# Reordered group work in the first expert layer of an FFT convolution with two dense layers, on one core

## The chip, the cores and the metric

The kernel runs on one core of a Trainium2 chip. The metric is the device time of one execution in microseconds (us), lower is better. The core's engines are TensorE (PE in the profile; its weight loads are PEld), VectorE (DVE), ScalarE (ACT), GpSimd (POOL), and SyncE (SP), which here only issues transfers. Each engine works through its own queue in the order of the program; an instruction that waits holds back all that stands behind it in the same queue.

## The reference

`x` has the shape (2, 3008, 256). It is filtered along the sequence by a product of Fourier transforms, and the 6016 tokens then pass two dense layers with 2048 hidden units each.

```python
X = np.fft.rfft(x, axis=1)
y = np.fft.irfft(X * (filt_r + 1j * filt_i), n=3008, axis=1)
x = y.reshape(6016, 256)
h = x @ moe_w_in                                   # 256 -> 2048
g = where(h >= 1, h, where(h <= -1, 0, (h + 1)**2 / 4))
x = g @ moe_w_out                                  # 2048 -> 256
h = x @ moe2_w_in
g = h / (1 + exp(-h))
return g @ moe2_w_out
```

The weights of both layers come as 64-bit floats, read as pairs of words. Every product is made from operands that are split in two rounded parts, high (h) and low (l): three matmuls, high by high, high by low and low by high, stand for one.

## The kernel before, in words

**Stages.** The first 340 us hold the transforms, the weights of the first layer and the first half of that layer's tokens, one unit of 128 hidden columns and about 500 tokens per slot of the agenda (`up`, `act_rest`, `split_g`, `down`). From slot `GA` (368.92 us in the profiled execution) on, the work goes in *groups*: nine pairs of token blocks (`PL`: three pairs of the first layer, `p` 0 to 2, then six of the second, `p` 3 to 8) times eight pairs of hidden units (`j`), so 72 groups, called G0 to G71 here (G = 8p + j). G0 to G23 are the first layer's, called wide; G24 to G71 the second layer's.

**A group (`group`, line 607).** Seven products in Strassen's manner stand for the eight block products of a pair of token blocks with a pair of hidden units. They are made in three PSUM banks `b`, `d`, `c` out of a ring of four (tag `h` of the pool `hp`; `load_pair` and `up` use the same ring): the first product and two more add up in `b`, two in `c`, one in `d`. Between them stand bank copies on ACT (`snap`: s1, u2, u4, line 546) and additions on DVE (c11 line 623, c22 line 661, c21 line 678), which give the four blocks 11, 22, 12 and 21. PE's order in a group is A11 and A12 into b and d, two matmul sets of the previous group's block 11 (line 387 on, six matmuls), S2 into b, block 22's six, S3 into c, S1 into b, block 12's six, S4 into b, A22 into c, block 21's six: 45 matmuls. S4 into b follows the copy u4; A22 into c follows the addition c22; the next group's d takes the bank that this group's b had, so it follows the last reading of b, which is block 12's activation.

**A block's chain (`Chain`).** `first` (ACT, line 565), `square` (ACT, 569), `last` (DVE, 574), `high` (the rounding, ACT, 582) and `low` (the remainder, DVE, 585); the block's six matmuls take the outputs of the last two. In a wide group the chains of blocks 22, 12 and 21 end in the next group. The blocks lie in a ring of three buffers (`block`, line 549).

**The agenda.** `at(t, fn)` puts a function at slot `t`; `due(t)` issues it. In the groups a group has four slots, and `between[i]` issues one block's six matmuls and then what is due in slot `GA + 4 * G + i`. What stands there: the first layer's weight sums (`sum_first` on DVE: six additions; `round_first` on ACT: two roundings; `rest_first` on POOL: two remainders), the same for the second layer's weights (`get_weight`: transfers on SP's queue; `sum_weight`, `round_weight`, `rest_weight`: four additions, three roundings, three remainders), and the next pair's tokens (`load_pair`, `sum_x` on DVE line 523, `split_x2` on ACT line 528, `rest_x2` on DVE line 533). The weights' staging tiles (tag `wa`) are a ring of three buffers.

**Around G0.** `up` and `down` slots GA - 16 to GA - 1 hold one unit each, 12 matmuls. DVE has in each slot the remainder gl (line 375) and the activation g (line 367), which frees a bank of the ring; the last four of these banks become b, d, c of G0 and b of G1. The same stretch also holds the last four weight conversions of the second layer (`form_weight`, lines 179 to 182, three DVE and one POOL instruction each, in slots GA - 10, - 8, - 6 and - 4), and the first pair's loading, sums and splits.

**Evictions.** When a pair's last group is done, its two output blocks are copied out (`evict`, line 391): each as one copy on ACT with its store on ACT's queue, and one on DVE with its store on SP's. The copies lie in a ring of four buffers (tag `ob`), from which each pair's operand T2 takes one too.

Of the kernel before, what the change touches and what calls it, by code (L numbers as in the profile page):

```python
# [9 lines left out]
F32 = mybir.dt.float32  # L10
# [82 lines left out]
def tile_fft_conv_moe_moe(  # L93
# [297 lines left out]
    def evict(o, name, to):  # L391
        for e in range(2):
            ob = mp.tile([128, PMAX], F32, tag="ob", name=f"ob{name}_{e}", bufs=4)[:, :o[e].shape[1]]
            if e == 0:
                nc.scalar.activation(ob, o[e], AF.Copy)  # L395
                nc.scalar.dma_start(to[e], ob)
            else:
                nc.vector.tensor_copy(ob, o[e])
                nc.sync.dma_start(to[e], ob)
# [91 lines left out]
    def load_pair(p):  # L491
        m, q = PL[p]
        n = size(p)
        for k in range(2):
            xstage[p, k] = mp.tile([128, 2 * n], F32, tag="x", name=f"xs{p}_{k}")
            if m == 1:
                t0 = BLOCKS[2 * q][0]
                nc.sync.dma_start(xstage[p, k], x2d[k, :, t0:t0 + 2 * n])
        if m == 0:
            for i in range(2):  # L500
                for k in range(2):
                    to = xstage[p, k][:, i * n:(i + 1) * n]
                    ps = last_stage(2 * q + i, k)
                    if k == 0:
                        nc.scalar.activation(to, ps, AF.Copy)
                    else:
                        nc.vector.tensor_copy(to, ps)

    def operand(p, which):

        n = size(p)
        if which == "T2":
            if (p, which) not in xstage:
                xstage[p, which] = mp.tile([128, PMAX], F32, tag="ob", name=f"t2_{p}", bufs=4)
            return xstage[p, which][:, :n]
# [33 lines left out]
    def block(p, j, name):  # L549
        return late.tile([128, PMAX], F32, tag="c", name=f"c{name}{p}_{j}", bufs=3)[:, :size(p)]  # L550

# [55 lines left out]
    def group(p, j, prev, between):  # L607
# [8 lines left out]
        if pwide:  # L616
            prev["22"].high()
            prev["22"].low()
            prev["12"].high()
# [3 lines left out]
        nc.vector.tensor_tensor(c11, d, s1, ALU.add)  # L623
        if pwide:
            prev["12"].low()
        if prev:
# [21 lines left out]
        k11.last()  # L648
        if pwide:
            prev["21"].high()  # L650
        between[1]()
        c = bank(p, j, "c")
        prod(c, p, j, "S3", "T3", True)
        prod(b, p, j, "S1", "T1", False)
        u4 = snap(b, p, j, "u4")
        if wide:
            k11.high()
        if pwide:
            prev["21"].low()
        c22 = block(p, j, "22")  # L660
        nc.vector.tensor_tensor(c22, c, u4, ALU.add)  # L661
        if wide:
# [86 lines left out]
    for j in range(NP):  # L749
        at(GA - 4 + 4 * j, sum_first, j)  # L750
        at(GA - 3 + 4 * j, round_first, j)
        at(GA - 2 + 4 * j, rest_first, j)
    zw = []
# [22 lines left out]
    for j in range(NP):  # L776
        t = Y - 24 + 4 * j + (4 if j > 2 else 0)
        for i in range(2):
            at(t - 2 + i, get_weight, 2 * j + i)
        at(t, sum_weight, j)  # L780
        at(t + 1, round_weight, j, store)
        at(t + 2, rest_weight, j)

# [12 lines left out]
    at(GA - 14, make_ring)  # L796
    first = {"B11": -11, "B21": -10, "T2": -7, "T3": -5, "T1": -3, "B22": -1, "T4": 0}
    sums = {"T1": -9, "T2": -8, "T3": -6, "T4": -1}
    later = {"B11": 12, "B21": 14, "T2": 18, "T3": 28, "T1": 28, "B22": 29, "T4": 30}
    sums_later = {"T1": 16, "T2": 17, "T3": 20, "T4": 24}  # L800
    for p in range(len(PL)):
        t = GA + 4 * NP * (p - 1) if p else GA
        at(t + (3 if PL[p][0] else 7) if p else GA - 12, load_pair, p)
        for which, d in (sums_later if p else sums).items():
# [125 lines left out]
```

## Time and profile before

| | |
|---|---|
| three runs, us | 1163.71, 1163.79, 1160.23 (median 1163.71) |
| the profiled execution's own time, us | 1160.99 |
| its span from the first to the last instruction, us | 1159.2 |
| mean granted TensorE clock, as a share of full speed | 0.996 |
| PE busy, us | 1120.9 |
| ACT busy, us | 818.7 |
| DVE busy, us | 771.3 |

The profile is of one execution. A line of a timeline has the start and the length of an instruction in us, its engine, its line in the kernel, the operation, output and inputs with shapes, and how many stand behind one another (x2); in square brackets is the idle time of the engine just before it and what ended it. PE matmuls overlap: consecutive ones start about 0.227 us apart and are shown 0.39 us long.

### The profile page before, as it was taken

What the parts mean: (1) busy time and instruction counts of PE and PEld (TensorE: products, weight loads), DVE (VectorE), ACT (ScalarE), POOL (GpSimd) and SP (SyncE); (2) the same over time, 40 slices, a digit from 0 to 9 for tenths busy, and PEclk for the clock granted to TensorE, in tenths of its full rate; (3) what the DMA queues carried; (4) which work ended last, traced back from release to release, by engine and by line L of the source; (5) the groups of instructions that cost most, each with busy time, mean ns of one, the idle gap of its engine ahead of it and who ended that gap; (6) DMA issues with size and microseconds to landing.
All of it is one profiled execution on the core that took longest, in us unless ns stands there. A gap on an engine that the chain in (4) does not pass through costs nothing.

```text
span 1159.2 us, 14143 instructions
## 1 busy us (share of the span) xinstructions
PE 1120.9 (97%) x4931; PEld 903.5 (78%) x4931; DVE 771.3 (67%) x1226; ACT 818.7 (71%) x1515; POOL 250.8 (22%) x220
## 2 busy tenths in 40 slices
PE   9899999999998998999999899999999999999998
PEld 4477787878887876788777678888888888888887
DVE  7977657878759788767778765545555555555443
ACT  3588777878866677878888776666666666666655
POOL 5677535657512111000021320000000000000000
PEclk9999999999999999999999999999999999999999
DMA  9732042444231000000120120110200200200000
GB/s 239 207 107 94 1 129 69 134 123 135 82 110 55 19 0 1 36 1 1 54 82 19 33 103 1 37 35 1 72 1 1 72 1 1 72 1 1 36 1 35
DMA packets 35591, 63.67 MB, mean 55 GB/s; under 512 B 4064, under 2 KB 18624, under 8 KB 35520
## 3 DMA queue, kind: packets, MB, share of 16 engines
q1 hardware_dynamic: 31808, 56.38, 16.2%
q10 hardware_dynamic: 3712, 6.40, 1.5%
q8 instruction: 38, 0.62, 0.2%
q14 instruction: 33, 0.27, 0.1%
HBM read 46.25 MB, written 16.52 MB: 54 GB/s over the span
## 4 chain that ended last, share of the span: by engine, by line
PE 77%; DVE 9%; ACT 7%; DMA 2%; issue 2%; POOL 2%; SPq 0%; DVEq 0%; ACTq 0%; POOLq 0%
PE o L387 13%; PE o L389 12%; PE o L388 12%; PE b L537 5%; PE b L538 5%; PE b L539 5%; PE h L354 3%; PE h L356 3%; PE h L355 3%; PE c L537 3%; PE xp L326 2%; PE c L538 2%; PE c L539 2%; DVE gl L585 1%; ACT gh L582 1%
## 5 line engine op out<-in xcount | busy, mean ns | idle before, releaser
L387 PE MATMUL o<-gh,wh 128*128 128x502 f32 (+1 forms) x624 | 245.4, 393 | 0.5 <-ACT ob L395 0.3
L389 PE MATMUL o<-gh,wl 128*128 128x502 f32 (+1 forms) x624 | 244.8, 392 | 0.0
L388 PE MATMUL o<-gl,wh 128*128 128x502 f32 (+1 forms) x624 | 244.6, 392 | 0.0
L585 DVE TENSOR_TENSOR gl<-c,gh 128x502 fp32r<-128x502 f32 (+1 forms) x288 | 195.5, 693 | 61.4 <-ACT gh L582 60.9
L582 ACT ACTIVATE gh<-c 128x502 fp32r<-128x502 f32 (+1 forms) x288 | 170.2, 617 | 11.7 <-DVE c L574 8.9
L546 ACT ACTIVATE u<-b 128x502 f32<-128x502 f32 (+1 forms) x144 | 83.8, 582 | 95.9 <-PE b L539 95.7
L387 PEld LDWEIGHTS o<-gh,wh 128*128 128x128 f32 x624 | 118.5, 190 | 26.4 <-ACT ob L395 1.0
L389 PEld LDWEIGHTS o<-gh,wl 128*128 128x128 f32 x624 | 118.3, 190 | 24.8
L388 PEld LDWEIGHTS o<-gl,wh 128*128 128x128 f32 x624 | 118.5, 190 | 24.3
L661 DVE TENSOR_TENSOR c<-c,u 128x502 f32<-128x502 f32 (+1 forms) x72 | 48.9, 679 | 100.9 <-ACT u L546 100.9
L561 ACT ACTIVATE c<-c 128x502 f32<-128x502 f32 (+1 forms) x144 | 88.6, 616 | 26.8 <-DVE c L661 26.2
L375 DVE TENSOR_TENSOR gl<-g,gh 128x502 fp32r<-128x502 f32 (+1 forms) x80 | 64.7, 809 | 51.5 <-ACT gh L373 51.4
L373 ACT ACTIVATE gh<-g 128x502 fp32r<-128x502 f32 (+1 forms) x96 | 59.8, 622 | 54.8 <-PE o L389 32.2
L678 DVE TENSOR_TENSOR c<-c,u 128x502 f32<-128x502 f32 (+1 forms) x72 | 48.9, 680 | 68.8 <-PE c L539 68.6
L546 ACT ACTIVATE s<-b 128x502 f32<-128x502 f32 (+1 forms) x72 | 42.5, 590 | 68.9 <-PE b L539 68.9
L354 PE MATMUL h<-xh,wh 128*128 128x502 f32 (+1 forms) x192 | 76.7, 399 | 3.8 <-DVE g L367 3.8
L367 DVE SCALAR_TENSOR_TENSOR g<-u,h 128x502 f32<-128x502 f32 (+1 forms) x96 | 64.2, 669 | 23.8 <-ACT u L366 23.8
L356 PE MATMUL h<-xh,wl 128*128 128x502 f32 (+1 forms) x192 | 75.1, 391 | 1.3 <-POOL wl L198 1.3
L355 PE MATMUL h<-xl,wh 128*128 128x502 f32 (+1 forms) x192 | 74.9, 390 | 0.0
L623 DVE TENSOR_TENSOR c<-d,s 128x502 f32<-128x502 f32 (+1 forms) x72 | 49.0, 680 | 32.9 <-PE d L539 23.8
L182 POOL TENSOR_TENSOR wa<-wa,raw 128x512 int32<-128x512 int32 x32 | 50.3, 1573 | 78.9 <-DVE wa L181 34.8
L360 ACT ACTIVATE u<-h 128x502 f32<-128x502 f32 (+1 forms) x96 | 55.5, 578 | 13.0 <-PE h L356 12.5
(197 smaller groups left out, 2405.0 us busy)
## 6 DMA issues: line engine op xcount, KB each, us to landing
f<-in_filt_dram SPq DMA_DIRECT2D x64, 192.0 KB, 4.6
raw<-in_moe_w_in_dram SPq DMA_DIRECT2D x32, 256.0 KB, 2.7
raw<-in_moe_w_out_dram SPq DMA_DIRECT2D x32, 256.0 KB, 3.1
w2d<-wa SPq DMA_DIRECT2D x16, 256.0 KB, 3.4
wb<-w2d SPq DMA_DIRECT2D x16, 256.0 KB, 2.8
xs<-x2d SPq DMA_DIRECT2D x8, 502.0 KB, 4.9
Z<-in_x_dram SPq DMA_DIRECT2D x16, 192.0 KB, 6.1
x<-in_x_dram SPq DMA_DIRECT2D x16, 192.0 KB, 3.6
```

Of the source, the lines that this page charges most:

```text
L354: nc.tensor.matmul(h, wh[:, s], xh[:, k, :t], start=(k == 0), stop=False)
L355: nc.tensor.matmul(h, wh[:, s], xl[:, k, :t], start=False, stop=False)
L356: nc.tensor.matmul(h, wl[:, s], xh[:, k, :t], start=False, stop=(k == 1))
L387: nc.tensor.matmul(o[e], wh[:, s], gh, start=first, stop=False)
L388: nc.tensor.matmul(o[e], wh[:, s], gl, start=False, stop=False)
L389: nc.tensor.matmul(o[e], wl[:, s], gh, start=False, stop=last)
L537: nc.tensor.matmul(bank, wh, xh, start=first, stop=False, skip_group_check=True)
L538: nc.tensor.matmul(bank, wh, xl, start=False, stop=False, skip_group_check=True)
L546: nc.scalar.activation(v, src, AF.Copy)
L561: nc.scalar.activation(self.g, self.h, AF.Silu)
L582: nc.scalar.activation(self.gh, self.g, AF.Copy)
L585: nc.vector.tensor_tensor(self.gl, self.g, self.gh.bitcast(F32), ALU.subtract)
```

## The change

In a group that follows a wide one, the remainder of the previous group's block 22 goes behind the addition c11, the rounding of its block 21 behind the copy u4, and the remainder of that block behind the addition c22. The block buffers become four and the eviction buffers three. `sum_first`, `round_first` and `rest_first` go from slots 0, 1, 2 of the group before (for j = 0: GA - 4, - 3, - 2) to slots 0, 2, 3 of the group before that one (j = 0: GA - 14, - 11, - 10; j = 1: GA - 6, - 5, - 4). `sum_weight` and its followers go from eight of the nine groups G18 to G26 (one per group, none in G21) to G18, G20, G22, G24, G25, G26, G27 and G28, the rounding in slot 2 in place of 1 and the remainder in slot 3 in place of 2. The first pair's loading goes from one slot to two, one slot earlier, and its sums and splits go earlier by one to six slots.

```diff
@@ -390,7 +390,7 @@
 
     def evict(o, name, to):
         for e in range(2):
-            ob = mp.tile([128, PMAX], F32, tag="ob", name=f"ob{name}_{e}", bufs=4)[:, :o[e].shape[1]]
+            ob = mp.tile([128, PMAX], F32, tag="ob", name=f"ob{name}_{e}", bufs=3)[:, :o[e].shape[1]]
             if e == 0:
                 nc.scalar.activation(ob, o[e], AF.Copy)
                 nc.scalar.dma_start(to[e], ob)
@@ -496,22 +496,24 @@
             if m == 1:
                 t0 = BLOCKS[2 * q][0]
                 nc.sync.dma_start(xstage[p, k], x2d[k, :, t0:t0 + 2 * n])
-        if m == 0:
-            for i in range(2):
-                for k in range(2):
-                    to = xstage[p, k][:, i * n:(i + 1) * n]
-                    ps = last_stage(2 * q + i, k)
-                    if k == 0:
-                        nc.scalar.activation(to, ps, AF.Copy)
-                    else:
-                        nc.vector.tensor_copy(to, ps)
+
+    def load_block(p, i):
+
+        n = size(p)
+        for k in range(2):
+            to = xstage[p, k][:, i * n:(i + 1) * n]
+            ps = last_stage(2 * PL[p][1] + i, k)
+            if k == 0:
+                nc.scalar.activation(to, ps, AF.Copy)
+            else:
+                nc.vector.tensor_copy(to, ps)
 
     def operand(p, which):
 
         n = size(p)
         if which == "T2":
             if (p, which) not in xstage:
-                xstage[p, which] = mp.tile([128, PMAX], F32, tag="ob", name=f"t2_{p}", bufs=4)
+                xstage[p, which] = mp.tile([128, PMAX], F32, tag="ob", name=f"t2_{p}", bufs=3)
             return xstage[p, which][:, :n]
         i, half = {"B11": (0, 0), "B12": (0, 1), "B21": (1, 0), "B22": (1, 1),
                    "T1": (0, 0), "T3": (0, 1), "T4": (1, 0)}[which]
@@ -547,7 +549,7 @@
         return v
 
     def block(p, j, name):
-        return late.tile([128, PMAX], F32, tag="c", name=f"c{name}{p}_{j}", bufs=3)[:, :size(p)]
+        return late.tile([128, PMAX], F32, tag="c", name=f"c{name}{p}_{j}", bufs=4)[:, :size(p)]
 
     class Chain:
 
@@ -615,13 +617,13 @@
         s1 = snap(b, p, j, "s1")
         if pwide:
             prev["22"].high()
-            prev["22"].low()
             prev["12"].high()
         d = bank(p, j, "d")
         prod(d, p, j, "A12", "B21", True)
         c11 = block(p, j, "11")
         nc.vector.tensor_tensor(c11, d, s1, ALU.add)
         if pwide:
+            prev["22"].low()
             prev["12"].low()
         if prev:
             prev["21"].first()
@@ -646,19 +648,19 @@
         if pwide:
             prev["21"].last()
         k11.last()
-        if pwide:
-            prev["21"].high()
         between[1]()
         c = bank(p, j, "c")
         prod(c, p, j, "S3", "T3", True)
         prod(b, p, j, "S1", "T1", False)
         u4 = snap(b, p, j, "u4")
+        if pwide:
+            prev["21"].high()
         if wide:
             k11.high()
+        c22 = block(p, j, "22")
+        nc.vector.tensor_tensor(c22, c, u4, ALU.add)
         if pwide:
             prev["21"].low()
-        c22 = block(p, j, "22")
-        nc.vector.tensor_tensor(c22, c, u4, ALU.add)
         if wide:
             k11.low()
         between[2]()
@@ -747,9 +749,10 @@
     GA = NB + W1S
     Y = GA + 4 * NP * (len(PAIRS) - NS // 2)
     for j in range(NP):
-        at(GA - 4 + 4 * j, sum_first, j)
-        at(GA - 3 + 4 * j, round_first, j)
-        at(GA - 2 + 4 * j, rest_first, j)
+        t, r = ((GA - 14, 3), (GA - 6, 1))[j] if j < 2 else (GA + 4 * (j - 2), 2)
+        at(t, sum_first, j)
+        at(t + r, round_first, j)
+        at(t + r + 1, rest_first, j)
     zw = []
 
     def store(j):
@@ -774,12 +777,12 @@
         at(t + 3, form_weight, 1, f)
         at(t + 5, put_weight, f)
     for j in range(NP):
-        t = Y - 24 + 4 * j + (4 if j > 2 else 0)
+        t = Y - 24 + 8 * j if j < 3 else Y + 4 * (j - 3)
         for i in range(2):
             at(t - 2 + i, get_weight, 2 * j + i)
         at(t, sum_weight, j)
-        at(t + 1, round_weight, j, store)
-        at(t + 2, rest_weight, j)
+        at(t + 2, round_weight, j, store)
+        at(t + 3, rest_weight, j)
 
     def make_ring():
         xr = zp.tile([128, 8, 2, 512], F32R, tag="z0", name="xr")
@@ -794,13 +797,17 @@
         ring.extend(lambda i=i: extra(i) for i in range(2))
 
     at(GA - 14, make_ring)
-    first = {"B11": -11, "B21": -10, "T2": -7, "T3": -5, "T1": -3, "B22": -1, "T4": 0}
-    sums = {"T1": -9, "T2": -8, "T3": -6, "T4": -1}
+    first = {"B11": -12, "B21": -11, "T2": -8, "T3": -6, "T1": -5, "B22": -3, "T4": -2}
+    sums = {"T1": -10, "T2": -9, "T3": -8, "T4": -7}
     later = {"B11": 12, "B21": 14, "T2": 18, "T3": 28, "T1": 28, "B22": 29, "T4": 30}
     sums_later = {"T1": 16, "T2": 17, "T3": 20, "T4": 24}
     for p in range(len(PL)):
         t = GA + 4 * NP * (p - 1) if p else GA
-        at(t + (3 if PL[p][0] else 7) if p else GA - 12, load_pair, p)
+        s = t + (3 if PL[p][0] else 7) if p else GA - 13
+        at(s, load_pair, p)
+        if PL[p][0] == 0:
+            for i in range(2):
+                at(s + (0 if p else i), load_block, p, i)
         for which, d in (sums_later if p else sums).items():
             at(t + d, sum_x, p, which)
         for which, d in (later if p else first).items():
```

## Rows read from the trace of the kernel before

**Rows 1.** The page's first part: busy time of an engine, share of the span, instructions.

```profile
PE 1120.9 (97%) x4931; PEld 903.5 (78%) x4931; DVE 771.3 (67%) x1226; ACT 818.7 (71%) x1515; POOL 250.8 (22%) x220
```

**Rows 2.** The waits of PE: line, what it waited for, us in total, times, longest us.

```profile
PE b L537 <- ACT u L546: 15.0, 13, 1.6
...
PE c L537 <- DVE c L661: 2.6, 3, 1.4
```

**Rows 3.** Busy time by stretch: from:to, length, then busy time (instructions) of PE, PEld, DVE, ACT, POOL, granted clock, DMA share, GB/s. The stretches begin at the first matmul of G0, G1, G2, G8, G16, G18 and G24; the last one ends with G26.

```profile
368.92:386.53 17.61, 14.64 (x53) 11.49 (x51) 15.46 (x26) 11.70 (x24) 5.28 (x5) 0.81 0.04 16
386.53:403.76 17.23, 16.31 (x99) 14.07 (x97) 11.19 (x21) 10.59 (x21) 1.51 (x2) 1.00 0.08 30
403.76:474.08 70.32, 63.79 (x273) 50.16 (x272) 57.60 (x106) 55.39 (x107) 9.26 (x10) 1.00 0.00 1
474.08:563.71 89.63, 88.80 (x410) 73.03 (x408) 65.17 (x104) 71.24 (x132) 0.00 (x0) 1.00 0.03 12
563.71:584.08 20.37, 20.37 (x91) 16.93 (x90) 15.85 (x26) 17.36 (x33) 0.00 (x0) 1.00 0.43 140
584.08:655.66 71.58, 64.05 (x271) 51.00 (x270) 58.58 (x99) 59.55 (x112) 21.05 (x15) 0.98 0.12 34
655.66:689.10 33.44, 31.32 (x136) 25.06 (x135) 21.00 (x39) 25.23 (x47) 11.18 (x9) 1.00 0.27 93
```

**Rows 4.** The chain of work that ended last, in order of time: start, us, step. One step of it, the 48 small matmuls of a pair's loading.

```profile
333.88 5.30 PE xp L326 x48
```

**Rows 5.** Timeline of G17, a group with nothing due: first matmul, the copy u4, S4's first matmul, and block 12's last DVE step.

```profile
573.91 0.38 PE L537 MATMUL b<-xr,wh 128*128 128x500 f32 x1
...
580.21 0.59 ACT L546 ACTIVATE u<-b 128x500 f32<-128x500 f32 x1
...
581.36 0.39 PE L537 MATMUL b<-xr,sh 128*128 128x500 f32 x1
...
583.58 0.67 DVE L574 SCALAR_TENSOR_TENSOR c<-v,b 128x500 f32<-128x500 f32 x1
```

**Rows 6.** Timeline of G3, a group with a weight sum: its first matmul, the sum's first additions, the last steps of blocks 21 and 11, the rounding of block 21, the first of the weight's two roundings, the copy u4, and S4's first matmul.

```profile
415.24 0.38 PE L537 MATMUL b<-xr,wh 128*128 128x502 f32 x1
...
419.23 0.76 DVE L451 TENSOR_TENSOR wr<-wh,wl 128x256 f32<-128x256 f32 x2
...
421.27 1.27 DVE L574 SCALAR_TENSOR_TENSOR c<-v,c 128x502 f32<-128x502 f32 x2
421.98 0.62 ACT L582 ACTIVATE gh<-c 128x502 fp32r<-128x502 f32 x1 [0.87 <-DVE c L574]
...
422.51 0.51 ACT L441 ACTIVATE sh<-ws 128x384 fp32r<-128x384 f32 x1
423.12 0.57 ACT L546 ACTIVATE u<-b 128x502 f32<-128x502 f32 x1
...
423.74 0.50 PE L537 MATMUL b<-xr,sh 128*128 128x502 f32 x1 [0.83 <-ACT u L546]
```

**Rows 7.** Timeline in G15 (a token rounding ahead of u4, two token remainders ahead of c22, A22's first matmul) and in G18 (a second-layer weight's three roundings on ACT and its first two remainders on POOL).

```profile
558.80 0.60 ACT L528 ACTIVATE xr<-xs 128x500 fp32r<-128x500 f32 x1
559.01 1.26 DVE L533 TENSOR_TENSOR xr<-xs,xr 128x500 fp32r<-128x500 f32 x2
...
561.51 0.50 PE L537 MATMUL c<-xr,wh 128*128 128x502 f32 x1 [0.62 <-DVE c L661]
...
590.47 1.13 ACT L441 ACTIVATE wz<-wb 128x512 fp32r<-128x512 f32 x2
591.16 2.53 POOL L444 TENSOR_TENSOR wz<-wb,wz 128x512 fp32r<-128x512 f32 x2 [130.58 <-ACT wz L441]
591.51 0.51 ACT L441 ACTIVATE sh<-ws 128x384 fp32r<-128x384 f32 x1
```

**Rows 8.** Timeline around the first matmuls of G0, DVE, POOL and PE: two remainders gl with DVE's idle time before each, the POOL addition of the last weight conversion, the remainder gl beside that, a POOL remainder, the activation g of slot GA - 3, and d's first matmul.

```profile
358.30 0.68 DVE L375 TENSOR_TENSOR gl<-g,gh 128x500 fp32r<-128x500 f32 x1 [0.75 <-ACT gh L373]
...
365.19 0.68 DVE L375 TENSOR_TENSOR gl<-g,gh 128x500 fp32r<-128x500 f32 x1 [0.75 <-ACT gh L373]
...
370.05 1.51 POOL L182 TENSOR_TENSOR wa<-wa,raw 128x512 int32<-128x512 int32 x1 [7.32 <-DVE wa L181]
370.33 1.75 DVE L375 TENSOR_TENSOR gl<-g,gh 128x500 fp32r<-128x500 f32 x1
371.52 1.43 POOL L444 TENSOR_TENSOR sl<-ws,sh 128x384 fp32r<-128x384 f32 x1
372.01 0.66 DVE L367 SCALAR_TENSOR_TENSOR g<-u,h 128x500 f32<-128x500 f32 x1
...
372.73 0.79 PE L537 MATMUL d<-xr,wh 128*128 128x502 f32 x1 [2.97 <-DVE g L367]
```

**Rows 9.** Busy time by stretch behind that matmul (columns as in rows 3).

```profile
373.70:378.40 4.70, 4.70 (x13) 3.71 (x12) 4.29 (x8) 3.83 (x8) 0.00 (x0) 0.50 0.00 0
```

**Rows 10.** Timeline: the idle time of PE ahead of S4 in G24.

```profile
664.84 0.49 PE L537 MATMUL b<-xr,sh 128*128 128x502 f32 x1 [1.50 <-ACT u L546]
```

**Rows 11.** Timeline of the end: the store of the first of the last four copies, and the last copy on DVE.

```profile
1154.03 0.34 ACTq L396 DMA_DIRECT2D out_dram<-ob_11p  x1
...
1155.44 0.68 DVE L398 COPY ob_10p<-o 128x500 f32<-128x500 f32 x1 [0.67 <-PE o L389]
```

**Rows 12.** The list of transfers: queue, count, KB each, us from issue to landing.

```profile
out_dram<-ob_11p ACTq DMA_DIRECT2D x1, 250.0 KB, 2.0
```

## The prediction

> **What bounds the kernel now.** The busy shares come first [rows 1]: PE is busy for 1120.9 us of a span of 1159.2, so at most some 38 us can be won without fewer matmuls, and the change takes none away. Next, who ends PE's idle times [rows 2]: 13 waits of S4 into b for the copy u4 on ACT take 15.0 us, 3 waits of A22 into c for the addition c22 take 2.6. Last, where: the stretches from G0 to G26 [rows 3]. G16 and G17 take 20.37 us, 10.2 a group, 45 matmuls without a gap; a pair's loading adds 5.3 [rows 4]. What each stretch has above that is the excess:
>
> G0: 17.61 less 51 matmuls of 0.227 (11.6) is 6.0. G1: 17.23 - 10.2 - 5.3 = 1.7. G2 to G7: 70.32 - 61.2 = 9.1. G8 to G15: 89.63 - 81.6 - 5.3 = 2.7. G16, G17: none. G18 to G23: 71.58 - 61.2 = 10.4. G24 to G26: 33.44 - 30.6 = 2.8. Together 32.7 us: all that the change can touch, since nothing it moves lies later, but for the buffers.
>
> The mechanism is read from a quiet and a loaded group. In G17 u4 starts 6.30 after the group's first matmul, and S4 7.45 after it, on time [rows 5]. In G3 u4 starts at 7.88 and S4 0.83 late [rows 6]: DVE's weight sum holds it from 3.99 to 6.03, so the last step of block 21 comes late, its rounding ends an ACT idle time of 0.87 at 6.74, the weight's roundings follow, and u4 stands behind all of them. PE waits for an order of work, not for a full engine: in G2 to G7 ACT is busy for 55.39 of 70.32 us, DVE for 57.60 [rows 3].
>
> **The change part by part.** *Copy u4 ahead of block 21's rounding, weight roundings to slot 2.* In G1 to G24 ACT can start u4 as soon as b is done, at 6.3; it takes 0.59, and S4 is due at 7.45. So the wait of S4 goes, with 0.5 to spare. c22 follows at 6.95 to 7.6, A22 is due at 8.15.
>
> What is late next is the start of d. Block 12's last step reads b, and the next group's d takes that bank. In G17 block 12's last DVE step ends at 10.34 [rows 5]; d is due at 10.2 + 0.68 = 10.88, so 0.54 is spare. Whatever now stands on ACT between the rounding of block 11 and block 22's first step (R) moves that chain. Where R is over 0.54, d is late by R - 0.54, and I add 0.15 for the restart. A first-layer weight's two roundings are 0.61 (422.51 to 423.12) [rows 6]: a wait of 0.2. With one token rounding (0.60, of which 0.53 start to start) it is 0.75. A second-layer weight's three are 1.55 (590.47 to 592.02) [rows 7]: 1.15; with a token rounding 1.7.
>
> By group: G1 keeps 0.4, since the next pair's loading stands ahead of G2's d. G2 and G5 0.2 each, G3 and G4 0.75 each (a token rounding is due in their slot 2), G6 has no weight left, G7 below: 2.6 in place of 9.1 with G7. G18 1.15, G19 0, G20 1.7, G21 0, G22 1.15. G24 has 0.5, its chain's second-layer form reading b in its first step; G25 and G26 none, where the roundings stand behind u4 and ACT is less full (25.23 of 33.44 us) [rows 3]: 0.5 in place of 2.8.
>
> *Token splits.* In G7, G15 and G23 two token remainders (1.26 on DVE) precede c22 and a token rounding (0.60) precedes u4 [rows 7]. Neither moves. In G15 A22 starts 0.62 late; block 21's remainder (0.6) stood behind the two and goes behind c22, but what the splits themselves cost ACT and DVE stays, and with it the start of the next d. I keep 0.7 in each of the three, of bounds 0.1 and 1.3. With 0.6 for the small rests in G8 to G14, G8 to G15 keep 1.3; G18 to G23 keep 1.15 + 1.7 + 1.15 + 0.7 = 4.7.
>
> *Block 22's remainder behind c11, block 21's behind c22.* Nothing is added; each comes later by one or two DVE steps of 0.6 to 0.7. Block 22's low matmuls are due at 3.63 and its remainder would end at about 2.85; block 21's are due at 9.07 and its remainder would end at 8.2. Cost nothing while that cover of 0.8 holds; without it, see the slower rival. The fourth block buffer is what lets c11 go ahead of the remainder that frees the buffer of block 22.
>
> *A port shared by DVE and POOL.* A POOL addition at 370.05 lasts until 371.56, and the remainder gl that DVE issues at 370.33 takes 1.75 in place of 0.68; the activation g with one input in PSUM takes its normal 0.66 beside POOL's next remainder [rows 8]. The Trainium skill, SBUF — State Buffer, "Who interferes with whom", says that whichever of the two starts first holds the shared pair for its whole instruction when DVE has two SBUF inputs, and that a DVE operation with one does not contend. By that rule the weights' remainders, now issued at about 8.4, would delay block 11's remainder only if it started after them; I have it at 8.15, so nothing. Were it the other way round, c21 and block 12's last step would come behind it, 0.35 in each of some nine groups: 3 us more.
>
> *Around G0.* d waits for g of slot GA - 3, 2.97 us [rows 8]. Between slot GA - 10 and that g DVE keeps four weight conversions, four token remainders and one weight sum (j = 1's for j = 0's) and gets one token sum more (0.6). The weight sum comes two slots sooner and fills DVE's two idle times of 0.75: -1.5. A POOL remainder now falls before that g and can hold a DVE remainder: between 0 and 1.43 [rows 8]; I take 0.5. So g is 0.4 earlier, bounds 0.9 earlier (POOL holds nothing) and 2.0 later (no idle time filled, POOL's whole 1.43), and PE idles for 2.6. Behind the 2.97 the granted clock was 0.50 of full, 1.2 GHz, for 13 matmuls and more [rows 9], which makes the other 2.9 of the 6.0; behind a single 1.50 in G24 PE goes on without such a stretch [rows 10], and the stretch of G24 to G26 has a clock of 1.00 [rows 3]. 2.6 is nearer to 2.97: I let the clock fall, and G0 keeps 5.6. If it does not, 2.9 more are won.
>
> *Eviction buffers, three.* Each pair's fourth copy now takes the buffer of its first and waits for that store. At the end of a pair's other groups the two are some 3 us apart, and a store lands after 2.0 [rows 12]: no wait. Behind the last matmul they are not: store issued at 1154.03, landed at 1156.03, the copy was at 1155.44 [rows 11]. The end comes 0.6 to 0.7 later; I take 0.7.
>
> **Sum.** What stays is 5.6 + 0.4 + 2.6 + 1.3 + 4.7 + 0.5 + 0.7 = 15.8, against 32.7: 16.9 less. The profiled execution's own time is 1160.99 (span 1159.2 and 1.8 around it); it lies 2.7 below the median of the three runs and beside the lowest. 1160.99 - 16.9 = 1144.1; I forecast 1144.
>
> **The rivals.** *The waits move to d and are no shorter (14 in 100).* If ACT's steps behind u4 come later than I have them, or POOL holds DVE as above, d waits for block 12 in every loaded group. G2 to G7 keep 5, G18 to G23 8, G0 its 6.0: 15.8 + 2.4 + 3.3 + 0.4 + 1 = 22.9 stays, 1151. For it: S4's wait today covers d's. Against it: the idle ACT time of 0.87 in front of block 21's rounding is gone in any case.
>
> *The clock stays up in G0 and d's waits are hidden (10 in 100).* G0 keeps 2.7 and the waits for d half: about 9 stay, 1137. For it: the first pair's work begins sooner. Against: no less DVE work before that g.
>
> *The stalls are work, not order (7 in 100).* Then ACT is late whatever the order, and the time stays between 1158 and 1164. Against it stand the quiet groups and the busy times [rows 3].
>
> *The deferred remainder of block 21 comes too late (7 in 100): slower.* Its low matmuls stand at the end of each group. From 0.9 later than my 8.2, PE waits there; every group from G1 to G24 pays, the nine quiet ones too. At 0.7 of wait a group, 24 x 0.7 = 16.8 eat the whole gain; at 1.0 the time is 1144 + 24 = 1168. For it: it now stands behind u4, two roundings and c22. Against: ACT and DVE are idle for parts of that stretch in G17.
>
> **How the numbers follow.** The forecast has 62 in 100, from 1138 to 1150 with the clock in G0 and the bounds above. A difference of 0.3% (3.5 us) is about what can be told here. Faster is the forecast and the first two rivals, 86; the same 7; slower 7. The range 1136 to 1156 leaves out the last two and the far end of the second, some 17 in 100.
>
> **What would show it.** Right: no wait of PE for u4 in G1 to G23, waits of about 1 to 1.7 of d for block 12's last step in G19, G21 and G23 (behind G18, G20, G22), half a granted clock after d in G0 still, a last DVE copy that waits for a store. Wrong: waits in front of block 21's low matmuls, any gap in G16 or G17, or waits of d behind groups without weight work.

## The result, and the profile after

The changed kernel takes 1143.93 us (median of four runs, 1143.57 to 1145.48), the kernel before beside it 1163.53 (1160.23 to 1163.79): a ratio of 0.9841, 95% interval 0.9821 to 0.9861. The prediction was 1144, range 1136 to 1156, with 86 in 100 for faster. The profiled execution takes 1143.57 us against 1160.99, so 17.4 less, where 16.9 was worked out. The sum is right; its terms are not all, as the stages show.

The windows by stage of the changed kernel stand in the same order as [rows 3]: G0, G1, G2 to G7, G8 to G15, G16 and G17, G18 to G23, G24 to G26; then G0 to G26 together, and from G27 to the end.

```profile
369.51:385.52 16.01, 12.11 (x52) 9.47 (x51) 13.04 (x23) 10.92 (x23) 3.10 (x3) 1.00 0.05 17
385.52:401.52 16.00, 16.00 (x98) 14.21 (x97) 10.73 (x21) 10.35 (x20) 1.68 (x2) 1.00 0.09 33
401.52:465.24 63.72, 62.62 (x273) 50.78 (x273) 53.96 (x99) 55.19 (x105) 7.87 (x8) 1.00 0.00 1
465.24:553.58 88.34, 88.04 (x410) 73.19 (x409) 64.46 (x104) 70.79 (x132) 0.00 (x0) 1.00 0.04 12
553.58:574.12 20.54, 20.54 (x91) 16.83 (x90) 16.16 (x27) 17.31 (x33) 0.00 (x0) 1.00 0.41 139
574.12:638.89 64.77, 62.89 (x272) 50.23 (x270) 50.59 (x88) 55.94 (x106) 11.13 (x9) 1.00 0.07 21
638.89:671.09 32.20, 31.49 (x137) 25.22 (x135) 22.15 (x41) 24.82 (x48) 10.94 (x9) 1.00 0.34 108
369.51:671.09 301.58, 293.69 (x1323) 239.92 (x1321) 231.10 (x398) 245.32 (x463) 34.72 (x31) 1.00 0.10 32
671.09:1141.80 470.71, 466.15 (x2050) 386.00 (x2048) 250.50 (x393) 303.91 (x551) 8.33 (x7) 1.00 0.07 24
```

The first number behind the window is its length; less 10.2 for each group (11.58 for G0, and 5.3 more where a pair is loaded) it gives the excess, as in the prediction:

| stage | before | predicted | after |
|---|---|---|---|
| G0 | 6.0 | 5.6 | 4.4 |
| G1 | 1.7 | 0.4 | 0.5 |
| G2 to G7 | 9.1 | 2.6 | 2.5 |
| G8 to G15 | 2.7 | 1.3 | 1.4 |
| G16, G17 | 0 | 0 | 0.1 |
| G18 to G23 | 10.4 | 4.7 | 3.6 |
| G24 to G26 | 2.8 | 0.5 | 1.6 |
| together | 32.7 | 15.1 | 14.1 |

That is 18.6 less in G0 to G26 (320.18 us before, 301.58 after). The part from G27 on takes 0.6 more (470.10 before), and G0 starts 0.6 later (368.92 before): 18.6 - 0.6 - 0.6 = 17.4. That G0 starts later is no work of the change: the first matmul of `up` starts at 58.66 before and at 59.38 after, so the shift is there long ahead of the first slot that the change touches. In the profiles of the kernels below G0 starts between 368.2 and 374.7, whatever their edit. Experiments are therefore compared by the length of G0 to G26, and totals by their medians.

What PE waits for in G0 to G26 answers to [rows 2]. The columns are the total in us, how many times, the longest.

```profile
PE d L539 <- DVE g L367: 2.3, 1, 2.3
PE c L539 <- DVE c L661: 2.2, 5, 0.7
...
PE b L539 <- issue: 1.6, 1, 1.6
...
PE o L388 <- DVE gl L587: 0.6, 1, 0.6
...
PE b L539 <- ACT u L548: 0.4, 1, 0.4
...
PE b L539 <- ACT s L548: 0.3, 1, 0.3
```

The wait for the copy u4, 13 times and 15.0 us before, is there once, for 0.4, in G23. The addition c22 is waited for five times, 2.2 in all (G4, G7, G15, G23, G25). d waits once, in G0 and for g; there is no wait of d for block 12, which the prediction had put into ten groups.

G3 shows what became of the mechanism in [rows 6]. Its timeline after the change (the group's first matmul is at 411.88):

```profile
418.23 0.59 ACT L548 ACTIVATE u<-b 128x502 f32<-128x502 f32 x1 [0.47 <-PE b L541]
...
418.72 1.12 ACT L584 ACTIVATE gh<-c 128x502 fp32r<-128x502 f32 x2
...
419.39 0.39 PE L539 MATMUL b<-xr,sh 128*128 128x502 f32 x1
```

u4 starts at +6.35, where it was +7.88, and what ends ACT's idle time in front of it is PE's last matmul into b: it is as early as it can be. Block 21's rounding follows behind it as one of the two at 418.72, and S4 comes at +7.51 with no idle time in front.

### The profile page after: what moved, and what is told of

The parts are those of the page before. It is cut to its first block, busy times and chain, and to the rows that moved or that the text cites. A ratio compares the mean times of both kernels' runs of the same rounds, so it can differ in the third digit from the quotient of the medians.

```text
span 1141.8 us, 14135 instructions
## 1 busy us (share of the span) xinstructions
PE 1114.9 (98%) x4931; PEld 901.7 (79%) x4931; DVE 765.1 (67%) x1226; ACT 817.0 (72%) x1515; POOL 249.5 (22%) x220
## 4 chain that ended last, share of the span: by engine, by line
PE 82%; DVE 6%; ACT 4%; issue 2%; POOL 1%; DMA 0%; ACTq 0%; DVEq 0%; SPq 0%; POOLq 0%
PE o L388 14%; PE o L387 14%; PE o L389 14%; PE b L539 5%; PE b L541 5%; PE b L540 5%; PE h L354 3%; PE c L539 3%; PE h L356 3%; PE h L355 3%; PE c L541 3%; PE c L540 3%; PE xp L326 3%; PE d L539 1%; PE d L540 1%
## 5 line engine op out<-in xcount | busy, mean ns | idle before, releaser
L587 DVE TENSOR_TENSOR gl<-c,gh 128x502 fp32r<-128x502 f32 (+1 forms) x288 | 191.0, 691 | 40.0 <-ACT gh L584 39.8
L576 DVE SCALAR_TENSOR_TENSOR c<-v,c 128x502 f32<-128x502 f32 (+1 forms) x72 | 49.2, 690 | 22.7 <-ACT v L571 22.4
```

What stands on the lines that cost most here:

```text
L587: nc.vector.tensor_tensor(self.gl, self.g, self.gh.bitcast(F32), ALU.subtract)
```

## Experiments

Ten runs follow. The first three tell apart where the gain comes from, the next five test the places where something was left, and the last two put together what helped and repeat the changed kernel.

**1. The order inside the groups alone.** The kernel before with the new order in `group` and the new buffer counts; the agenda stays as it was.

```diff
             prev["22"].high()
-            prev["22"].low()
             prev["12"].high()
...
         u4 = snap(b, p, j, "u4")
+        if pwide:
+            prev["21"].high()
         if wide:
             k11.high()
+        c22 = block(p, j, "22")
+        nc.vector.tensor_tensor(c22, c, u4, ALU.add)
         if pwide:
             prev["21"].low()
```

> The kernel before with the new order inside a group and the new buffer counts, its agenda left as it was. Theory (order): PE waited because u4 stood behind block 21's rounding; with u4 ahead, the waits of S4 for u4 in G1 to G6 nearly go although the weight sums and roundings stay in their old slots. Left: G0's 6.0, some 0.5 for each second-layer weight whose three roundings (1.45) still stand ahead of u4, 0.8 at the end. About 20 of the 32.7 us of excess stay: 1148, between 1145 and 1152. Rival (agenda): the weight work in the same group is what costs; then this run stays within 4 us of the kernel before, 1156 to 1161.

Measured: 1152.81 us (1151.47 to 1153.45), ratio 0.9930, interval 0.9914 to 0.9947. G0 to G26 take 310.89 us: 9.3 of the 18.6. The waits of PE in that stretch, as above:

```profile
PE c L537 <- DVE c L659: 5.1, 8, 1.3
...
PE b L537 <- ACT u L546: 3.3, 5, 1.6
```

Most of the 13 waits for u4 go by the order alone. But 8 waits for c22 with 5.1 us take the place of 3 with 2.6. In G3 to G6 they do not come from u4, which starts there at +6.4, on time: DVE is late. Out of G3:

```profile
419.13 1.22 POOL L444 TENSOR_TENSOR sl<-ws,sh 128x384 fp32r<-128x384 f32 x1 [8.67 <-PE b L539]
419.15 0.57 ACT L546 ACTIVATE u<-b 128x502 f32<-128x502 f32 x1
...
419.39 1.50 DVE L533 TENSOR_TENSOR xr<-xs,xr 128x502 fp32r<-128x502 f32 x1
...
420.81 0.67 DVE L659 TENSOR_TENSOR c<-c,u 128x502 f32<-128x502 f32 x1
```

A token remainder on DVE starts 0.26 behind a POOL remainder of the weight, which the old agenda has in slot 2, and takes 1.50 where two take 1.26 elsewhere [rows 7]. c22 follows it without idle time, 1.09 after the end of u4. In G0 to G26 of this run 24 steps of DVE last over 0.8 us, together some 17 us more than at their usual 0.67; in the kernel before there are 16 with some 8 us, in the changed kernel 6 with some 4. That is DVE's time and not PE's, but it shows what the agenda adds here: it takes POOL's remainders out of the way of the steps ahead of c22. In G18 to G25 the second-layer roundings in slot 1 stand ahead of u4 as well. The expectation was too good.

**2. The agenda alone.** The other half: the changed kernel with the old order in `group` and the old buffer counts.

```diff
+            prev["22"].low()
             prev["12"].high()
...
+        if pwide:
+            prev["21"].high()
         between[1]()
...
         u4 = snap(b, p, j, "u4")
-        if pwide:
-            prev["21"].high()
```

> The changed kernel with the old order inside a group and the old buffer counts: the agenda's moves alone. Theory (order): with a weight sum still in slot 0, u4 comes at about 7.3 behind block 21's rounding and S4 waits some 0.5 in each of G1 to G5, 1.0 where a token sum stands there too; the second-layer weights gain by being spread. About 18 us of excess stay: 1146, between 1143 and 1151; the two parts alone add up to more than the change, since either removes the roundings from ahead of u4. Rival (the order does it all): within 3 us of the kernel before.

Measured: 1152.09 us (1151.43 to 1155.48), ratio 0.9933, interval 0.9918 to 0.9949; G0 to G26 308.40, so 11.8 of the 18.6. Waits for u4 remain six times with 3.1, for c22 eight times with 3.7, so this expectation, too, was too good. Neither half is the change: 9.3 + 11.8 = 21.1 against 18.6 together, so each takes away some of the stalls that the other would. The rival, under which the agenda alone gives almost nothing, falls.

**3. The second layer's weights back in their old slots.** All else as changed.

```diff
-        t = Y - 24 + 8 * j if j < 3 else Y + 4 * (j - 3)
+        t = Y - 24 + 4 * j + (4 if j > 2 else 0)
...
-        at(t + 2, round_weight, j, store)
-        at(t + 3, rest_weight, j)
+        at(t + 1, round_weight, j, store)
+        at(t + 2, rest_weight, j)
```

> The changed kernel with the second layer's weight sums, roundings and remainders in their old slots. Theory: three roundings of together 1.45 stand ahead of u4 again, in six groups, two of them on end with token splits; G18 to G26 go from some 5 us of excess to 9 to 11: 1148 to 1150. Rival: the new order gives ACT room enough, and the spread is worth under 1.5: 1143 to 1145.

Measured: 1150.67 us (1149.80 to 1154.26), ratio 0.9921, interval 0.9905 to 0.9937. G18 to G26 take 102.49 us against 64.77 + 32.20 = 96.97, so 5.5 more; G0 to G17 take 204.61 in both. The waits in G0 to G26:

```profile
PE c L539 <- DVE c L661: 3.4, 5, 1.3
...
PE b L539 <- ACT u L548: 3.3, 5, 1.6
```

The u4 waits come back, 3.3 in place of 0.4, in the loaded groups of that stage alone. With the roundings in slot 1 the order u4 first doesn't help, since they stand ahead of it. So 5.5 of the 18.6 hang on where this work stands. The run moves the slots and the groups together and doesn't tell them apart.

**4. The last four weight conversions moved out of G0's approach**, into slot 3 of the groups G8 to G11, which have no weight work. Their raw words now all go through the one buffer with the tag `raw`.

```diff
+        elif m == 1:
+            raw = rawp.tile([128, 512], I64, tag="raw", name=f"raw{m}_{f}", bufs=1)
...
-        t = NB + (34 + 4 * f if f < EARLY else 83 + 2 * (f - EARLY))
+        t = NB + 34 + 4 * f if f < EARLY else GA + 4 * (8 + f - EARLY)
```

> The changed kernel with the last four weight conversions of the second layer moved from the slots ahead of G0 into G8 to G11, one in each. Theory: in G0 d waits for g, and S2 for s1, because DVE is behind by the four conversions (1.4 each, and a POOL addition beside each that holds one remainder for 1.1). Both waits go, G0 falls from 4.4 of excess to under 1; the conversions cost up to 0.5 in each of their new groups: 1139 to 1142. Rival (the token sums and remainders put DVE behind): G0 keeps 3 or more, 1143 to 1146.

Measured: 1144.16 us (1142.82 to 1144.86), ratio 0.9858, interval 0.9843 to 0.9872: no gain in the total, and G0 to G26 take 303.03, 1.5 more. The windows of G0 and of G9, where most of the price falls:

```profile
369.23:380.91 11.68, 11.68 (x52) 9.53 (x51) 8.07 (x16) 7.83 (x16) 1.59 (x2) 1.00 0.00 1
470.87:490.28 19.41, 17.63 (x94) 14.78 (x93) 13.08 (x21) 12.88 (x24) 2.58 (x2) 0.91 0.26 89
```

G0 loses its whole excess (11.68 us for 51 matmuls at 0.227), so the backlog from the conversions is its cause, and the rival, the token work, falls. The 4.3 won there are lost in G9 (19.41 in place of 15.69, with a pair's loading in both), G11 (0.65 more) and G12 (1.33 more), 5.7 together. G9 pays twice: PE is idle for 1.78 of the 19.41 (19.41 less 17.63), and it is busy for 17.63 where the changed kernel has 15.69, because the granted clock falls (0.91 in the whole of G9, 0.50, which is 1.2 GHz, from 478.00 to 480.00). So about half of G9's price is the lower clock. One of the waits ahead of that fall, from its timeline:

```profile
474.84 1.30 POOL L184 TENSOR_TENSOR wa<-wa,raw 128x512 int32<-128x512 int32 x1 [35.12 <-ACT s L550]
...
475.13 2.15 DVE L589 TENSOR_TENSOR gl<-c,gh 128x502 fp32r<-128x502 f32 x2
...
476.74 0.49 PE L390 MATMUL o<-gl,wh 128*128 128x502 f32 x1 [1.04 <-DVE gl L589]
```

Two remainders that take 1.26 elsewhere [rows 7] take 2.15 here, behind a POOL addition that began 0.29 before them, and PE waits 1.04 for the first. This is the port shared by DVE and POOL that the prediction read in [rows 8]. The Trainium skill, SBUF — State Buffer, "Who interferes with whom", says that the one that issues first has the pair for its whole instruction and blocks the other; this timeline agrees, with 0.9 lost where the addition had 1.01 still to go. For G0 the expectation holds, but the price of the move was set too low.

**5. Block 22's remainder ahead of c11 again**, all else as changed.

```diff
             prev["22"].high()
+            prev["22"].low()
             prev["12"].high()
...
         if pwide:
-            prev["22"].low()
             prev["12"].low()
```

> The changed kernel with block 22's remainder back ahead of c11. Theory: the new waits of block 22's low matmuls in G19, G21 and G23 (0.30, 0.83, 0.29) come from the second-layer weight's three roundings one group earlier, which make block 22's last step and so its rounding late, with c11 (0.6) put ahead of its remainder on top; they shrink to 0, about 0.25 and 0, and G18 to G23 lose some 1 us, while the quiet groups stay at 10.2. Rival: the wait only moves to c11's followers; G18 to G23 stay within 0.3.

One run: 1143.26 us; G18 to G26 take 96.72 against 96.97, so the rival holds. In G21 PE's wait for the low matmuls goes from 0.61 to 0.22, but the excess only from 0.95 to 0.80; in G19 (0.75) and G23 (1.85) it stays. So where this remainder stands among DVE's steps is worth about nothing, neither as a gain of the change nor as a cost.

**6. The last copy into a buffer that is free.**

```diff
-            ob = mp.tile([128, PMAX], F32, tag="ob", name=f"ob{name}_{e}", bufs=3)[:, :o[e].shape[1]]
+            tag, bufs = ("g", 2) if e == 1 and name == "1_10p" else ("ob", 3)
+            ob = mp.tile([128, PMAX], F32, tag=tag, name=f"ob{name}_{e}", bufs=bufs)[:, :o[e].shape[1]]
```

> The changed kernel with the very last copy in a buffer of another ring, so that it needn't wait for a store. Theory: DVE's idle time before that copy falls from 1.49 to 0.67 as before the change, and the stretch from the first matmul of G27 to the end of the span falls from 470.7 by 0.8, to 469.9. Rival: the end hangs on the transfers, which then queue behind one another; it stays within 0.3 of 470.7.

One run: 1145.03 us, with G0 starting 1.5 later than in the changed kernel's profile, so only the stretch from G27 on can be compared: 470.30 against 470.71, 0.4 less. The last copy, first as changed and then here, each from its own timeline:

```profile
1138.09 0.68 DVE L398 COPY ob_10p<-o 128x500 f32<-128x500 f32 x1 [1.49 <-DMA out_dram<-ob_11p]
```

```profile
1139.39 0.68 DVE L399 COPY ob_10p<-o 128x500 f32<-128x500 f32 x1 [0.68 <-PE o L389]
```

The releaser changes from the store to PE, and the idle time from 1.49 to 0.68, that of before [rows 11]. The wait costs 0.8 at its place, and the end gets it back: from the first matmul of the last group, G71, to the end of the span it is 19.58 us before the change, 20.35 after it and 19.61 here. The whole stretch shows only 0.4 because G27 to G29, which the edit doesn't touch, take 0.1 each longer in this profile, as they do in the second profile of the changed kernel (experiment 10).

**7. The token work later.** Sums, splits and remainders of the next pairs go where they no longer stand ahead of c22.

```diff
-    later = {"B11": 12, "B21": 14, "T2": 18, "T3": 28, "T1": 28, "B22": 29, "T4": 30}
-    sums_later = {"T1": 16, "T2": 17, "T3": 20, "T4": 24}
+    later = {"B11": 12, "B21": 14, "T2": 19, "T3": 28, "T1": 28, "B22": 29, "T4": 30}
+    sums_later = {"T1": 16, "T2": 18, "T3": 24, "T4": 26}
+    lag = {"T3": 2, "T1": 3, "B22": 3, "T4": 2}
...
-            at(t + d + 1, rest_x2, p, which)
+            at(t + d + (lag.get(which, 1) if p else 1), rest_x2, p, which)
```

> The changed kernel with the next pair's token sums and remainders moved off the DVE slots ahead of c22 (T2's sum by one slot, T3's by four, T4's by two, the remainders of T3, T1, B22 and T4 by one or two). Theory: what is left of A22's waits for c22 (excess of 1.1 in G4, 0.4 in G5, 0.7 in G7, 0.7 in G15, and part of G23's 1.85) is DVE work issued between block 11's last step and c22; G4, G5, G7 and G15 fall to about 0.1 each, G23 by 0.5 or more, 3 us in all. Rival: the splits on ACT ahead of u4 make c22 late; then G7 and G15 keep 0.5 or more.

One run: 1142.09 us; G0 to G26 299.95, so 1.6 less. G4 goes from 1.12 to 0.56, G7 from 0.70 to 0.07, G15 from 0.68 to 0.10, G23 from 1.85 to 1.49, but G25 from 1.53 to 2.29. G4, first as changed:

```profile
430.02 0.67 DVE L525 TENSOR_TENSOR t<-xs,xs 128x502 f32<-128x502 f32 x1
...
430.61 0.67 DVE L661 TENSOR_TENSOR c<-c,u 128x502 f32<-128x502 f32 x1
...
431.34 0.49 PE L539 MATMUL c<-xr,wh 128*128 128x502 f32 x1 [0.74 <-DVE c L661]
```

```profile
429.91 0.67 DVE L661 TENSOR_TENSOR c<-c,u 128x502 f32<-128x502 f32 x1
...
430.64 0.50 PE L539 MATMUL c<-xr,wh 128*128 128x502 f32 x1 [0.15 <-DVE c L661]
```

A single token sum of 0.67 (line 525) stood between u4 and c22. In G7 and G15 the 0.7 was the token remainders ahead of c22, as predicted; of the expected 3 us 0.8 is given back in G25, and G4 and G23 keep more than was thought.

**8. The weight roundings one slot later still**, into slot 3, their remainders into the next group's slot 0.

```diff
-        at(t + 2, round_weight, j, store)
-        at(t + 3, rest_weight, j)
+        at(t + 3, round_weight, j, store)
+        at(t + 4, rest_weight, j)
```

> The changed kernel with the second-layer weights' roundings in slot 3 in place of 2 and their remainders in the next group's slot 0. Theory: the roundings stand ahead of blocks 22's and 12's first steps and so delay the next group; behind those steps ACT has about 0.9 of idle time, the excess of G19 (0.74), G21 (0.95) and G25 (1.53) falls to under 0.4 each: 2 us less. Rival: POOL's remainders then meet block 22's and 12's remainders at the start of the next group, and DVE waits for the shared port: G19 and G21 keep or exceed what they have.

One run: 1141.69 us; G0 to G26 299.56, so 2.0 less. By group it is mixed: G19 0.74 to 0.22, G23 1.85 to 1.08, G25 1.53 to 0.68, but G21 0.95 to 1.09, and outside the stretch G28 0.63 more. So the weight work in slots 2 and 3 holds G19, G23 and G25. In G21 the rival comes true: the remainders of blocks 22 and 12 take 1.18 and 1.48 on DVE, beside the weight's remainders on POOL, where they take 0.67 each in the changed kernel, and PE waits 0.81 for the first of them. G19 and G23 have the same two steps of 1.18 and 1.48, 0.8 earlier in the group, and there PE does not wait for them.

**9. What helped, together.** The changed kernel with the token work of 7, the roundings of 8 for the first four weights only, the conversions in slot 0 of four groups (G9, G10, G13 and G17), and the last copy of 6. The edits of 6 and 7, shown there, are left out here.

```diff
-        t = NB + (34 + 4 * f if f < EARLY else 83 + 2 * (f - EARLY))
+        t = NB + 34 + 4 * f if f < EARLY else GA + 4 * (9, 10, 13, 17)[f - EARLY] - 3
...
-        at(t + 2, round_weight, j, store)
-        at(t + 3, rest_weight, j)
+        at(t + (3 if j < 4 else 2), round_weight, j, store)
+        at(t + (4 if j < 4 else 3), rest_weight, j)
```

> The changed kernel with what the runs so far showed, together: the token work later, the second-layer weights' roundings in slot 3 for j under 4, the last four conversions in slot 0 of G9, G10, G13 and G17 (in place of slot 3 of G8 to G11), the last copy in another ring. Theory: G0 falls from 4.4 of excess to 0.1, the token work gives 1.9, the roundings 1.5, the end 0.4; the conversions cost under 0.5 each, since in slot 0 DVE and ACT have about 2 us of room, as a weight sum of 2.0 there shows in G2: 7 us less than the changed kernel, 1135 to 1138. Rival: POOL's addition holds a step of DVE wherever it stands, 1.2 in each of the four groups and a fallen clock in one of them, as in the run with the conversions in slot 3: 3 us less, 1139 to 1142.

Measured: 1135.17 us (1134.70 to 1137.17), ratio to the kernel before 0.9775, interval 0.9759 to 0.9790. G0 takes 11.69 us. The window of G0 to G26:

```profile
368.23:662.86 294.63, 292.58 (x1323) 239.86 (x1322) 237.42 (x404) 246.67 (x464) 39.28 (x34) 1.00 0.13 42
```

Of the 301.58 us 294.63 are left, and PE is idle for 2.1 of them. This beats both kernels, and the rival of 1139 to 1142 falls. What the rival says of POOL is there all the same: one step of DVE takes 1.65 to 1.79 in each of the four groups. But PE loses 0.70, 0.04, 0.27 and 0.61 in them, and not 1.2 in each.

**10. The changed kernel again**, on the same chip and beside the ninth.

> The changed kernel itself, beside the one above on the same chip: 1142 to 1146, its groups from G0 to G26 301.6 us as before, and G0 16.0 whether or not the clock falls behind d's wait.

Measured: 1143.98 us (1143.20 to 1144.99), ratio 0.9847, interval 0.9832 to 0.9862; the ninth kernel is 8.8 us faster than it. Its profile bears on G0. The windows of G0 and of the stretch behind d:

```profile
369.31:385.32 16.01, 13.66 (x53) 10.59 (x52) 13.04 (x23) 10.92 (x23) 3.11 (x3) 0.89 0.05 17
373.50:376.20 2.70, 2.70 (x8) 2.13 (x7) 2.54 (x5) 2.16 (x5) 0.00 (x0) 0.50 0.00 0
```

Here the granted clock does fall, to 0.50 of full, which is 1.2 GHz, where the first profile of the same kernel has 1.00. G0 lasts 16.01 us in both.

## Why the prediction was right, and where it was not

**Right: S4's wait goes.** u4 is late by the order of ACT's and DVE's work. Its waits fall from 15.0 us to 3.3 by the order inside the groups alone, to 3.1 by the agenda alone, and to 0.4 by both. The third experiment is the test: with the second layer's roundings back in slot 1 they return to 3.3. The rival that stalls are work and not order falls with it, and with the ninth, which does the same work with 2.1 us of idle time. The slower rival falls too: no group waits for block 21's low matmuls, and G16 and G17 take 20.54 us, 20.37 before, without a wait of PE in the list.

**Wrong: "What is late next is the start of d."** The prediction held that the next group's d takes the bank of b, and so waits for block 12's last step, by R - 0.54 + 0.15. The trace shows otherwise. Out of G20 and G21, after the change:

```profile
603.10 1.14 ACT L441 ACTIVATE wz<-wb 128x512 fp32r<-128x512 f32 x2
...
604.14 0.51 ACT L441 ACTIVATE sh<-ws 128x384 fp32r<-128x384 f32 x1
...
606.16 0.39 PE L539 MATMUL d<-xr,wh 128*128 128x500 f32 x1
...
606.83 0.68 DVE L576 SCALAR_TENSOR_TENSOR c<-v,b 128x500 f32<-128x500 f32 x1 [1.84 <-ACT v L571]
...
607.42 0.70 DVE L576 SCALAR_TENSOR_TENSOR c<-v,c 128x500 f32<-128x500 f32 x1
...
608.16 1.14 ACT L584 ACTIVATE gh<-c 128x500 fp32r<-128x500 f32 x2 [0.38 <-DVE c L576]
...
608.64 0.67 DVE L624 TENSOR_TENSOR c<-d,s 128x500 f32<-128x500 f32 x1
...
609.23 1.25 DVE L587 TENSOR_TENSOR gl<-c,gh 128x500 fp32r<-128x500 f32 x2
...
609.95 0.49 PE L388 MATMUL o<-gl,wh 128*128 128x500 f32 x1 [0.61 <-DVE gl L587]
```

G21's d starts at 606.16 with no idle time in front, and block 12's last step begins to read b only at 606.83 (the line with the input b). So d does not take that bank, and the description of the kernel ahead of the prediction, which says the same, is wrong there. The three roundings of a second-layer weight (603.10 to 604.65) do push ACT back, as R said; but what comes late is the next thing down that chain: block 22's last step at 607.42, its rounding at 608.16 behind 0.38 of idle ACT, its remainder behind c11 at 609.23, and then its low matmuls, late by 0.61. So the price was put in the right groups (behind G18, G20, G22) but at another matmul and larger than it is: with 1.15 + 1.7 + 1.15 forecast, and 0.7 for token splits in G23, G19 has 0.74, G21 0.95, and G23 1.85. That made G18 to G23 3.6 in place of 4.7. PE's idle time ahead of block 22's low matmuls is 0.61 in G21, but only 0.15 and 0.13 in G19 and G23; the larger waits of G23 are those for u4 (0.35) and c22 (0.55), behind a token rounding and two token remainders. What holds G21 is not settled by one edit: it has 0.87 with the token work later (experiment 7), 1.09 with the roundings later (8), and 0.43 with both (9).

**Hit with wrong terms: G2 to G7.** 2.6 was forecast and 2.5 measured, but by groups G3 has 0.08 where 0.75 stood, and G4 1.12 where 0.75 stood. G4's is a token sum on DVE ahead of c22, which the prediction did not price; experiment 7 takes half of it away. G7 and G15 have the 0.7 each that was kept for the token splits, and the same experiment takes nearly all of it.

**Mis-sized: G24 to G26, 0.5 forecast, 1.6 measured.** Nearly all is in G25 (1.53): waits of b for s1 and of c for c22. The step that failed is "G25 and G26 none, where the roundings stand behind u4 and ACT is less full": it looks at ACT, and for c22 it is DVE that is late, behind a transfer.

```profile
650.30 2.11 DVE L587 TENSOR_TENSOR gl<-c,gh 128x502 fp32r<-128x502 f32 x2 [1.65 <-ACT gh L584]
...
653.02 0.32 SPq L399 DMA_DIRECT2D x2d<-ob_10p  x1
653.43 0.38 SPq L190 DMA_DIRECT2D wb<-w2d  x1
...
656.19 0.29 DVE L434 TENSOR_TENSOR ws<-wb,wb 128x128 f32<-128x128 f32 x1 [2.03 <-DMA wb<-w2d]
...
658.70 0.49 PE L539 MATMUL c<-xr,wz 128*128 128x502 f32 x1 [0.29 <-DVE c L661]
```

Two remainders take 2.11 on DVE, beside POOL's remainders of a weight; DVE's eviction copy follows them, its store follows on SP's queue, and the transfer of the next weight stands behind that store. So the weight's sum on DVE waits 2.03 for the transfer, with block 11's remainder and c22 behind it. In experiment 8, where G25 has 0.68, the sum starts without idle time; in experiment 7, where two token remainders stand in G24 and G25 has 2.29, it waits 2.15 for its transfer.

**Wrong price: the fallen clock in G0.** The working was 2.6 of waiting and 2.9 for the lower clock, put at 5.6 (6.0 less 0.4). In the first profile after the change the wait is 2.32, the clock stays up, and the second of the two prices is still mostly paid:

```profile
372.68 0.49 PE L539 MATMUL d<-xr,wh 128*128 128x502 f32 x1 [2.32 <-DVE g L367]
...
376.74 0.62 ACT L373 ACTIVATE gh<-g 128x500 fp32r<-128x500 f32 x1 [0.88 <-DVE g L367]
...
377.27 0.57 ACT L548 ACTIVATE s<-b 128x502 f32<-128x502 f32 x1
...
377.94 0.47 PE L539 MATMUL b<-xr,sh 128*128 128x502 f32 x1 [1.58 <-issue]
```

PE reaches S2 early and then waits 1.58. The row names "issue", but S2 goes into b, and the copy s1 that reads b is issued behind a rounding that waited for DVE's g, and ends at 377.84, 0.10 before S2. DVE's backlog sets when G0 goes on, once at d and once at S2; a PE at half the clock in between arrives at the same time (experiment 10). The backlog is that of the weight conversions: experiment 4 takes G0 to 0.10 of excess. So the fall was forecast as a cost of its own where another chain covers it, and the rival that gave 2.9 for a clock that stays up was mis-sized in the same way.

**Right: the ends.** 0.7 was forecast for the wait that three eviction buffers bring. DVE is idle 0.8 longer ahead of the last copy, the part from G71 on takes 0.77 more (20.35 for 19.58), and a free buffer gives 0.74 of it back. The first two experiments agree: from G27 on the agenda alone, with the old buffer counts, takes 470.10 us as before, the order alone, with the new ones, 470.71.

**Nearly right: the port.** The prediction put the weights' remainders on POOL beside DVE's steps at nothing. Six steps of DVE in G0 to G26 still last over 0.8 us after the change, one of them in G0 beside a conversion; of the other five, only the one in G25 was followed to a wait of PE. What the prediction did not count is the gain: in the kernel before there are 16 such steps, and with the order alone 24 (experiment 1).

**A sum of errors.** The total came out to within 0.5 us of 17.4 because G0 and G18 to G23 were set too dear by 1.2 and 1.1, and G24 to G26 too cheap by 1.1, with G0's later start of 0.6 on top. That closeness is luck. The range, not the closeness, is what the working had earned.

## What to carry to other kernels

In an in-order kernel whose full engine waits on engines with idle time, look at what stands ahead of the copy that is waited for and move that behind it; then move the side work of the agenda behind it too, since either half alone brought only 9.3 and 11.8 of the 18.6. A wait that is read out of the program alone, like that of d for the bank of b, needs a rival in which it doesn't exist. The trace of before could not settle it: in G1 to G24 d always starts after block 12's last step has ended there, by 0.13 in G17, the least. Only a group in which that step is late, as in G21 after the change, tells. Side work moved out of one place needs slots with room on every engine and port that it uses: the same four conversions lost more than they won in G8 to G11 (5.7 for 4.3), and G9, G13 and G17 lose some 1.6 together where they stand in experiment 9.

## What the runs showed that was not expected

The same kernel with the same idle time of PE in front of G0's d shows the lower clock in one execution (0.50 in a stretch of 2.70 us) and not in the other (1.00 in the whole of G0). Which of the two it is changed nothing: G0 took 16.01 us in both, since PE waited for DVE and ACT anyway. Eight profiles have the new agenda and the conversions ahead of G0: five show a clock of 1.00 in G0 and three one of 0.89, and G0 takes between 15.97 and 16.07 us in all of them.

Stages that no edit touches differ by more than most of the edits are worth: G0 starts at 368.2 us in one profile and at 374.7 in another. In the later one, that of experiment 3, the granted clock is 0.91 in the first 60 us, where the changed kernel's first profile has 0.97 and the kernel before 1.00. A single total could not have ranked the edits of 0.4 to 2 us; the windows by stage could.
